# In the last row block, the first branch's sum of each column part is made ahead of the second branch's sum of the part before

## The chip, the cores and the metric

The kernel runs on one core of one Trainium2 chip. The metric is the device time in microseconds (us) of that core. All runs quoted are runs of the same program start to finish. Several runs of a kernel are told as their median, with the lowest and the highest.

A profile gives the span from the first to the last instruction, about 1.3 us shorter than the time. The views print times to 0.01 us. The distances behind PE's last matmul are taken from the ns of the trace and then rounded, so one can be 0.01 off the difference of two printed times. PE is TensorE (matmuls), ACT is ScalarE, DVE is VectorE, SP is the engine that issues most DMA transfers.

## The reference, cut to what matters

Two linear-attention branches, A and B, of the same shape are computed from the same 2048 x 640 input. A gate made from the input mixes them.

```python
x = A_x                                   # (1, 2048, 640) bf16
g = sigmoid((x * gate_w).sum(-1, keepdims=True))
a = branch(x, A_wqkv, A_wo)               # linear attention, then @ wo
b = branch(x, B_wqkv, B_wo)
return g * a + (1 - g) * b
```

By the time the output is made, the kernel has folded everything of a branch but the scaled query features into one 640 x 640 matrix `WP`. A block of 128 output rows is therefore `g * (PQ_A @ WP_A) + (1 - g) * (PQ_B @ WP_B)`, each product a sum of five matmuls over 128 features each. There are 16 row blocks.

## The kernel before

A small list scheduler in Python records every operation with what it reads and writes, and orders each engine's instructions before they are emitted. `final` records one row block. For each column part, PE makes A's sum and ACT scales it by `g` into a buffer `TS`. PE then makes B's sum, and DVE adds `(1 - g)` times it to `TS`. The first fifteen row blocks have one part of 640 columns. The last one has three, of 320, 160 and 160 columns, so that the work behind PE's last matmul is small:

```python
def final(t, parts=((0, D),), put=None):
    last = len(parts) > 1
    ...
    for lo, hi in parts:
        n = 1 if hi - lo <= 512 else 2
        w = (hi - lo) // n
        ts = _Tile(1, ring["ts"])                 # one of three TS slots
        ...                                        # o_ap, t_ap: the output and TS slices
        for x, X in enumerate(XS):                 # branch A, then branch B
            tile = _Tile(n)                        # PSUM bank(s)
            ...
            mms("f%s%d" % (X, t), steps, ...)      # PE: five matmuls per bank
            if x == 0:
                sch.op("ACT", lambda e, ...: e.activation(t_ap(), acc(), ACT.Copy, scale=GA[:, 0, t : t + 1]), ...)
            else:
                sch.op("DVE", lambda e, ...: e.scalar_tensor_tensor(
                    out=o_ap(), in0=acc(), scalar=GA[:, 1, t : t + 1], in1=t_ap(), op0=ALU.mult, op1=ALU.add), ...)
        ...                                        # the output transfer, where one is due

final(t, ((0, 320), (320, 480), (480, D)), {320: 0, D: 320})   # the last row block; two output transfers
```

I call the three parts 0, 1 and 2 and the sums A0, B0, A1 and so on. PE makes them in the order A0 B0 A1 B1 A2 B2.

Of the kernel before, what the change touches and what calls it, by code (L numbers as in the profile page):

```python
# [15 lines left out]
ACT = mybir.ActivationFunctionType  # L16
ALU = mybir.AluOpType
# [7 lines left out]
NC = 5  # L25
# [261 lines left out]
def _act_ns(n, psum=True):  # L287
    return n / 1.2 + (52.0 if psum else 94.0)


def _dve_ns(n, rate=1):
    return n / (0.96 * rate) + 68.0
# [6 lines left out]
def bass_gated_mix__linear_attn_block__linear_attn_block__prompt_kernel(nc, A_x, A_wqkv, A_wo, B_x, B_wqkv, B_wo, gate_w, out):  # L299
# [4 lines left out]
    XS = ("A", "B")  # L304

    with ExitStack() as es:
        E = es.enter_context

        def sb(name, shape, dtype=dt.bfloat16):
            return E(nc.sbuf_tensor(name, shape, dtype))  # L310
# [11 lines left out]
        PQ = {X: FE[:, x, :].rearrange("p (k s) -> p k s", s=S) for x, X in enumerate(XS)}  # L322
        WP = {X: sb("WP" + X, [128, NC, D]) for X in XS}
# [12 lines left out]
        GA = sb("GA", [128, 2, NT], dt.float32)  # L336
# [10 lines left out]
        OL = sb("OL", [128, D])  # L347
        OS = sb("OS", [128, NOS, D])
# [3 lines left out]
        PS = E(nc.psum_tensor("ps", [128, 8, 512], dt.float32))  # L352
# [4 lines left out]
        sch = _Sched()  # L357
# [5 lines left out]
        def dma(eng, name, dst, src, reads=(), writes=(), us=1.0, transpose=False, slow=False):  # L363
            n_sem[0] += 1
            sem = E(nc.semaphore(name="d%d_%s" % (n_sem[0], name)))

            def fn(e):
                if slow:
                    with nc.allow_non_contiguous_dma(reason="few elements"):
                        ins = e.dma_start(dst, src)  # L370
                else:
                    ins = e.dma_start(dst() if callable(dst) else dst, src() if callable(src) else src, transpose=transpose)  # L372
                return ins.then_inc(sem, 16)

            return sch.op(eng, fn, us * 1e3, reads=reads, writes=writes, name=name, sem=sem)

        def mms(name, steps, reads, writes, cols, lat=190.0, par=1, prio=None, after=None):


            def fn(pe):  # L380
                ins = None
                for o, l, r, a, z, tp in steps():
                    ins = pe.matmul(o, l, r, start=a, stop=z, tile_position=tp, skip_group_check=True)  # L383
                return ins

            return sch.op("PE", fn, cols / PE_GHZ / par, reads=reads, writes=writes, name=name, lat=lat, prio=prio, after=after)
# [39 lines left out]
        for t0, t1 in ((2, 4), (4, 8), (8, 12), (12, 16)):  # L426
            dma(
                "SP", "xt%d" % t0, XT[:, :, 128 * t0 : 128 * t1], xin[128 * t0 : 128 * t1, :],
                writes=[("XT", t) for t in range(t0, t1)], us=0.82 * (t1 - t0), transpose=True,
# [3 lines left out]
        for t0, t1 in ((2, 4), (4, 8), (8, 12), (12, 16)):  # L433
            dma(
                "SP", "xn_%d" % t0, XN[:, t0:t1, 0:D], xin[128 * t0 : 128 * t1, :].rearrange("(t p) f -> p t f", p=128),
                writes=[("XN", t) for t in range(t0, t1)], us=0.5 * (t1 - t0),
# [49 lines left out]
        ring = {"ek": _Ring(NEK), "dn": _Ring(2), "rx": _Ring(2), "os": _Ring(NOS), "ts": _Ring(NTS)}  # L486
# [335 lines left out]
        def final(t, parts=((0, D),), put=None):  # L822

            last = len(parts) > 1
            os = None if last else _Tile(1, ring["os"])
            row = out[0, 128 * t : 128 * t + 128, :]
            for lo, hi in parts:
                n = 1 if hi - lo <= 512 else 2
                w = (hi - lo) // n
                ts = _Tile(1, ring["ts"])  # L830

                def o_ap(lo=lo, hi=hi, w=w):
                    v = OL[:, lo:hi] if last else OS[:, os.slot, lo:hi]
                    return v.rearrange("p (h f) -> p h f", f=w)

                def t_ap(ts=ts, hi=hi, lo=lo, w=w):
                    return TS[:, ts.slot, 0 : hi - lo].rearrange("p (h f) -> p h f", f=w)

                okey = ("OL", lo) if last else (os,)
                for x, X in enumerate(XS):  # L840
                    tile = _Tile(n)

                    def steps(X=X, tile=tile, lo=lo, w=w, n=n):
                        return [
                            (PS[:, tile.banks[h], 0:w], PQ[X][:, k, 128 * t : 128 * t + 128],
                             WP[X][:, k, lo + w * h : lo + w * h + w], k == 0, k == NC - 1, None)
                            for k in range(NC) for h in range(n)
                        ]

                    def acc(tile=tile, n=n, w=w):  # L850
                        b0 = tile.banks[0]
                        return PS[:, b0 : b0 + n, 0:w]

                    mms(
                        "f%s%d" % (X, t), steps, [("PQS", X, t)] + [("WP", X, k) for k in range(NC)], [(tile,)], 5 * n * (w + 6),
                    )
                    if x == 0:
                        sch.op(
                            "ACT", lambda e, acc=acc, t_ap=t_ap: e.activation(t_ap(), acc(), ACT.Copy, scale=GA[:, 0, t : t + 1]),  # L859
                            _act_ns(hi - lo), reads=[(tile,), ("GA",)], writes=[(ts,)], name="fa%d" % t,  # L860
                        )
                    else:
                        sch.op(
                            "DVE",
                            lambda e, acc=acc, t_ap=t_ap, o_ap=o_ap: e.scalar_tensor_tensor(  # L865
                                out=o_ap(), in0=acc(), scalar=GA[:, 1, t : t + 1], in1=t_ap(), op0=ALU.mult, op1=ALU.add
                            ),
                            _dve_ns(hi - lo), reads=[(tile,), (ts,), ("GA",)], writes=[okey], name="fb%d" % t,
                        )
                p0 = (put or {}).get(hi, None if last else 0)  # L870
                if p0 is not None:
                    outs.append(dma(
                        "SP", "out%d_%d" % (t, lo), row[:, p0:hi],
                        (lambda p0=p0, hi=hi: OL[:, p0:hi]) if last else (lambda: OS[:, os.slot, :]),
                        reads=[("OL", c) for c, _ in parts if p0 <= c < hi] if last else [(os,)], us=0.4,
                    ))


        kt = {(X, t): _Tile(2) for X in XS for t in (0, 1)}
# [45 lines left out]
        def finals(b):  # L925
            for t in range(4 * b, 4 * b + 4):
                if t < NT - 1:
                    final(t)
                else:
                    final(t, ((0, 320), (320, 480), (480, D)), {320: 0, D: 320})  # L930
# [51 lines left out]
```

## Time and profile before

| | before |
|---|---|
| time, median of 3 runs | 190.69 us (190.65 to 190.99) |
| span of the profiled run | 189.5 us |
| PE busy | 185.9 us (98%) |
| PE's last matmul ends (modelled) | 187.26 us |
| the last DVE operation starts, ends | 187.51, 187.89 us |
| the last transfer, issue to landing | 1.6 us |

Two lines of the page show what bounds the kernel: the busy times with their shares of the span and the numbers of instructions, and the chain that ended last, by engine.

```profile
PE 185.9 (98%) x1289; PEld 124.0 (65%) x1289; DVE 129.8 (68%) x275; ACT 76.5 (40%) x129; POOL 8.2 (4%) x14
...
PE 94%; DMA 3%; SPq 1%; issue 0%; ACT 0%; DVE 0%; DVEq 0%; ACTq 0%
```

PE is the limit, and its share of the chain equals nearly the whole span. The chain in order of time (start, duration, what) shows where it leaves PE:

```profile
3.55 5.46 DMA WK<-in_B_wqkv_dram
...
9.05 177.88 PE ps L383 x1238
186.93 0.02 issue
186.95 0.02 ACTq L276
186.97 0.04 issue
187.01 0.40 ACT TS L859
187.42 0.03 issue
187.44 0.02 DVEq L276
187.47 0.04 issue
187.51 0.38 DVE OL L865
```

The chain is on PE from 9.05 us, when a weight load lands, until 186.93, when A2's sum ends. It then goes to ACT, which scales A2, and from there to the last DVE operation. Between the links stand short pieces called "issue", and the separate wait instructions (ACTq and DVEq, both L276). PE itself goes on to make B2 meanwhile.

The timeline shows that (start, duration, engine and line, operation, and in brackets the idle time before it with its releaser). A matmul group's start plus its duration is its modelled end.

```profile
186.06 0.51 PE L383 MATMUL ps<-WPB,FE 128*128 128x160 bf16 x5
...
186.41 0.51 PE L383 MATMUL ps<-WPA,FE 128*128 128x160 bf16 x5
...
186.75 0.51 PE L383 MATMUL ps<-WPB,FE 128*128 128x160 bf16 x5
...
187.01 0.39 ACT L859 ACTIVATE TS<-ps,GA 128x160 f32<-128x160 f32 x1 [0.36 <-PE ps L383]
187.51 0.38 DVE L865 SCALAR_TENSOR_TENSOR OL<-ps,GA,TS 128x160 bf16<-128x160 f32 x1 [0.37 <-ACT TS L859]
```

The matmuls of B2 are the line at 186.75 and end at 187.26. The last DVE operation has everything from PE by then and starts only at 187.51, because ACT works on A2 from 187.01 to 187.40. I call the distance from the end of PE's last matmul to the start of the last DVE operation the gap. Here it is 187.51 - (186.75 + 0.51) = 0.25 us. The waits of the last stretch (total, times, longest) put the DVE's largest share there to ACT:

```profile
DVE OL L865 <- ACT TS L859: 0.6, 2, 0.4
DVE OL L865 <- PE ps L383: 0.4, 1, 0.4
```

After DVE there is only the transfer. The view of the output buffer of the last block gives the DVE durations (minimum, median, maximum in ns) and the time to landing:

```profile
L865 DVE SCALAR_TENSOR_TENSOR OL<-ps,GA,TS x3: 383/384/552, 186.0 to 187.5; 128x160 bf16<-128x160 f32 x2, 128x320 bf16<-128x320 f32 x1
...
DMA to landing us min/median/max: 1.6/1.6/1.6
```

The record of an SP transfer lasts 0.33 us, while its landing takes 1.6. The Trainium skill ("Perfetto Trace Analysis", Summary: the profiler window per engine type) says that such a record leaves out the actual data movement. This trace agrees. So a microsecond and a half at the end of the span has no busy engine.

### The profile page before, as it was taken

How to read it: one execution, taken by the hardware profiler on the slowest of the kernel's cores; microseconds unless marked ns; L12 is line 12 of the kernel's file. 1: busy time of each engine (PE TensorE's matmuls, PEld its weight loads, DVE VectorE, ACT ScalarE, POOL GpSimd, SP SyncE). 2: the span in 40 equal slices, each digit the busy share in tenths (PEclk: the TensorE clock that was granted, in tenths of full speed). 3: DMA queues.
4: the chain of work that ended last, by engine and by line, in shares of the span. 5: the costliest groups of instructions: out<-in, count | busy, mean ns of one | idle time of the engine just before them, and what ended most of it. 6: DMA issues, size and time to landing. Idle time of an engine off the chain costs nothing.

```text
span 189.5 us, 3208 instructions
## 1 busy us (share of the span) xinstructions
PE 185.9 (98%) x1289; PEld 124.0 (65%) x1289; DVE 129.8 (68%) x275; ACT 76.5 (40%) x129; POOL 8.2 (4%) x14
## 2 busy tenths in 40 slices
PE   7999999999999999999999999999999999999995
PEld 2555555555788888888855666455556677777774
DVE  1398998999600009996179997898999959933324
ACT  2265656565311122103255478565553422332232
POOL 8900000000000000000000000000000000000000
DMA  5999699991011111112143004675000173221212
GB/s 189 298 243 177 211 388 364 337 231 33 0 35 38 35 35 38 35 35 38 35 95 102 5 22 173 166 224 170 0 0 3 44 226 92 86 89 35 73 69 69
DMA packets 31936, 21.49 MB, mean 113 GB/s; under 512 B 16818, under 2 KB 31666, under 8 KB 31922
## 3 DMA queue, kind: packets, MB, share of 16 engines
q1 hardware_dynamic: 31490, 20.80, 39.5%
q10 hardware_dynamic: 432, 0.49, 0.8%
q8 instruction: 10, 0.16, 0.4%
q14 instruction: 4, 0.03, 0.1%
HBM read 12.05 MB, written 5.31 MB: 92 GB/s over the span
## 4 chain that ended last, share of the span: by engine, by line
PE 94%; DMA 3%; SPq 1%; issue 0%; ACT 0%; DVE 0%; DVEq 0%; ACTq 0%
PE ps L383 94%; DMA WK<-in_B_wqkv_dram 3%; SPq L372 1%; ACT TS L859 0%; DVE OL L865 0%; DVEq L276 0%; ACTq L276 0%
## 5 line engine op out<-in xcount | busy, mean ns | idle before, releaser
L383 PE MATMUL ps<-WK,XT 128*128 128x512 bf16 (+2 forms) x250 | 44.0, 337 | 0.5 <-DMA WK<-in_A_wqkv_dram 0.2
L383 PE MATMUL ps<-XN,FE 128*128 128x320 bf16 x320 | 44.3, 300 | 0.0
L383 PEld LDWEIGHTS ps<-XN,FE 128*128 128x128 bf16 x320 | 37.5, 118 | 5.9
L383 PEld LDWEIGHTS ps<-WK,XT 128*128 128x128 bf16 x250 | 24.1, 98 | 20.0 <-DMA WK<-in_A_wqkv_dram 0.5
L743 ACT ACTIVATE EK<-ps 128x512 bf16<-128x512 f32 x40 | 23.9, 597 | 18.5 <-PE ps L383 16.9
L563 ACT ACTIVATE EK<-ps 128x512 bf16<-128x512 f32 (+1 forms) x42 | 21.4, 526 | 16.2 <-PE ps L383 16.2
L752 DVE SCALAR_TENSOR_TENSOR FE<-ps,EK 128x512 bf16<-128x512 f32 x40 | 26.8, 688 | 0.7
L859 ACT ACTIVATE TS<-ps,GA 128x640 f32<-128x640 f32 (+2 forms) x18 | 13.2, 734 | 29.5 <-PE ps L383 29.5
L383 PE MATMUL ps<-WPB,FE 128*128 128x320 bf16 (+1 forms) x165 | 24.7, 295 | 0.0
L383 PE MATMUL ps<-WPA,FE 128*128 128x320 bf16 (+1 forms) x165 | 24.7, 295 | 0.0
L573 DVE SCALAR_TENSOR_TENSOR FE<-ps,EK 128x512 bf16<-128x512 f32 (+1 forms) x42 | 23.9, 596 | 0.5
L865 DVE SCALAR_TENSOR_TENSOR OS<-ps,GA,TS 128x640 bf16<-128x640 f32 x15 | 13.0, 869 | 14.7 <-PE ps L383 14.7
L383 PE MATMUL ps<-XT,WQA 128*128 128x512 bf16 x100 | 22.8, 380 | 0.0
L383 PE MATMUL ps<-XT,WQB 128*128 128x512 bf16 x100 | 22.7, 379 | 0.0
L600 ACT ACTIVATE GS<-ps 128x640 bf16<-128x640 f32 x10 | 7.0, 704 | 37.0 <-PE ps L383 37.0
L383 PEld LDWEIGHTS ps<-WPA,FE 128*128 128x128 bf16 x165 | 15.9, 98 | 6.1
L383 PEld LDWEIGHTS ps<-WPB,FE 128*128 128x128 bf16 x165 | 15.8, 98 | 6.2 <-ACT TS L859 0.4
L383 PEld LDWEIGHTS ps<-XT,WQB 128*128 128x128 bf16 x100 | 11.7, 117 | 9.1
L383 PEld LDWEIGHTS ps<-XT,WQA 128*128 128x128 bf16 x100 | 11.6, 118 | 9.4 <-issue 0.4
L705 DVE SCALAR_TENSOR_TENSOR GP<-XN,GWB 128x640 bf16<-128x640 bf16 x16 | 13.3, 829 | 4.1 <-PE ps L383 3.6
L811 DVE TENSOR_TENSOR FE<-FE,RX 128x1280 bf16<-128x1280 bf16 (+1 forms) x20 | 12.6, 685 | 1.6 <-DMA RX<-factor 1.6
L567 DVE TENSOR_SCALAR EK<-EK 128x512 bf16<-128x512 bf16 (+1 forms) x42 | 11.4, 272 | 3.1
(52 smaller groups left out, 80.3 us busy)
## 6 DMA issues: line engine op xcount, KB each, us to landing
out_dram<-OS SPq DMA_DIRECT2D x15, 160.0 KB, 1.8
XN<-in_A_x_dram SPq DMA_DIRECT2D x3, 640.0 KB, 8.1
factor<-RC SPq DMA_DIRECT2D x4, 256.0 KB, 2.6
RX<-factor SPq DMA_DIRECT2D x4, 256.0 KB, 3.2
WVA<-in_A_wqkv_dram SPq DMA_DIRECT2D x1, 800.0 KB, 10.4
WQA<-in_A_wqkv_dram SPq DMA_DIRECT2D x1, 800.0 KB, 11.9
WVB<-in_B_wqkv_dram SPq DMA_DIRECT2D x1, 800.0 KB, 11.2
WQB<-in_B_wqkv_dram SPq DMA_DIRECT2D x1, 800.0 KB, 12.5
```

The lines of the kernel that those rows point to most:

```text
L372: ins = e.dma_start(dst() if callable(dst) else dst, src() if callable(src) else src, transpose=transpose)
L383: ins = pe.matmul(o, l, r, start=a, stop=z, tile_position=tp, skip_group_check=True)
L563: "ACT", lambda e, ps=ps, ek=ek: e.activation(ek(), ps(), ACT.Exp), _act_ns(n), reads=[(tile,)], writes=[(es,)],
L567: "DVE", lambda e, ek=ek: e.tensor_scalar(ek(), ek(), 1.0, EPS, op0=ALU.min, op1=ALU.add), _dve_ns(n, 4),
L573: return e.scalar_tensor_tensor(out=out, in0=two(ps()), scalar=0.0, in1=two(ek()), op0=ALU.max, op1=ALU.add)
L600: "ACT", lambda e: e.activation(GS[:, k, :].rearrange("p (h f) -> p h f", f=HALF), pair(tile, HALF), ACT.Copy),
L705: lambda e, t=t: e.scalar_tensor_tensor(out=GP[:, :], in0=XN[:, t, 0:D], scalar=1.0, in1=GWB[:, :], op0=ALU.mult, op1=ALU.mult, accum_out= ...
L743: "ACT", lambda e: e.activation(ek(), PS[:, tile.banks[0], :], ACT.Exp), _act_ns(512), reads=[(tile,)],
L752: lambda e: e.scalar_tensor_tensor(out=dst, in0=PS[:, tile.banks[0], :], scalar=0.0, in1=ek(), op0=ALU.max, op1=ALU.add),
L811: return e.tensor_tensor(out=v, in0=v, in1=RX[:, xs.slot, 512 * x + w * j : 512 * x + w * j + w].unsqueeze(1).to_broadcast([128, NC, w]), ...
L859: "ACT", lambda e, acc=acc, t_ap=t_ap: e.activation(t_ap(), acc(), ACT.Copy, scale=GA[:, 0, t : t + 1]),
L865: lambda e, acc=acc, t_ap=t_ap, o_ap=o_ap: e.scalar_tensor_tensor(out=o_ap(), in0=acc(), scalar=GA[:, 1, t : t + 1], in1=t_ap(), op0=ALU.m ...
```

## The change

The intent: make A's sum of the next part before B's sum of this part, so that ACT's scaling of A runs under PE's other work and the last DVE operation waits for PE alone. PE's order becomes A0 A1 B0 A2 B1 B2. The row blocks with one part stay as they were.

```diff
-            for lo, hi in parts:
+            got = {}
+
+            def total(x, lo, hi):
                 ...
-                ts = _Tile(1, ring["ts"])
+                X = XS[x]
+                tile = _Tile(n)
+                ts = got.setdefault(lo, _Tile(1, ring["ts"]))
                 ...
-                for x, X in enumerate(XS):
-                    tile = _Tile(n)
-                    ...
+                mms("f%s%d" % (X, t), steps, ...)
+                if x == 0:
+                    sch.op("ACT", ...)
+                    return
+                sch.op("DVE", ...)
                 ...                                # the output transfer, as before
+            for i, (lo, hi) in enumerate(parts):
+                if i == 0:
+                    total(0, lo, hi)
+                if i + 1 < len(parts):
+                    total(0, *parts[i + 1])
+                total(1, lo, hi)
```

No operation is added or removed. The built programs differ in the order of the last six groups of matmuls on PE, and the operations of ACT, DVE and SP keep their order.

More of the change, by code (lines that the diff above doesn't have):

```diff
@@ L826, in final, with steps, acc, o_ap @@
             row = out[0, 128 * t : 128 * t + 128, :]
-            for lo, hi in parts:
+            got = {}
+            def total(x, lo, hi):
                 n = 1 if hi - lo <= 512 else 2
                 w = (hi - lo) // n
-                ts = _Tile(1, ring["ts"])
-                def o_ap(lo=lo, hi=hi, w=w):
+                X = XS[x]
+                tile = _Tile(n)
+                ts = got.setdefault(lo, _Tile(1, ring["ts"]))
+                def steps():
+                    return [
+                        (PS[:, tile.banks[h], 0:w], PQ[X][:, k, 128 * t : 128 * t + 128],
+                         WP[X][:, k, lo + w * h : lo + w * h + w], k == 0, k == NC - 1, None)
+                        for k in range(NC) for h in range(n)
+                    ]
+                def acc():
+                    return PS[:, tile.banks[0] : tile.banks[0] + n, 0:w]
+                def o_ap():
@@ L833, in o_ap, with t_ap @@
                     v = OL[:, lo:hi] if last else OS[:, os.slot, lo:hi]
                     return v.rearrange("p (h f) -> p h f", f=w)
-                def t_ap(ts=ts, hi=hi, lo=lo, w=w):
+                def t_ap():
                     return TS[:, ts.slot, 0 : hi - lo].rearrange("p (h f) -> p h f", f=w)
-                okey = ("OL", lo) if last else (os,)
-                for x, X in enumerate(XS):
-                    tile = _Tile(n)
-                    def steps(X=X, tile=tile, lo=lo, w=w, n=n):
-                        return [
-                            (PS[:, tile.banks[h], 0:w], PQ[X][:, k, 128 * t : 128 * t + 128],
-                             WP[X][:, k, lo + w * h : lo + w * h + w], k == 0, k == NC - 1, None)
-                            for k in range(NC) for h in range(n)
-                        ]
-                    def acc(tile=tile, n=n, w=w):
-                        b0 = tile.banks[0]
-                        return PS[:, b0 : b0 + n, 0:w]
-                    mms(
-                        "f%s%d" % (X, t), steps, [("PQS", X, t)] + [("WP", X, k) for k in range(NC)], [(tile,)], 5 * n * (w + 6),
-                    )
-                    if x == 0:
-                        sch.op(
-                            "ACT", lambda e, acc=acc, t_ap=t_ap: e.activation(t_ap(), acc(), ACT.Copy, scale=GA[:, 0, t : t + 1]),
-                            _act_ns(hi - lo), reads=[(tile,), ("GA",)], writes=[(ts,)], name="fa%d" % t,
-                        )
-                    else:
-                        sch.op(
-                            "DVE",
-                            lambda e, acc=acc, t_ap=t_ap, o_ap=o_ap: e.scalar_tensor_tensor(
-                                out=o_ap(), in0=acc(), scalar=GA[:, 1, t : t + 1], in1=t_ap(), op0=ALU.mult, op1=ALU.add
-                            ),
-                            _dve_ns(hi - lo), reads=[(tile,), (ts,), ("GA",)], writes=[okey], name="fb%d" % t,
-                        )
@@ new lines, in total @@
+                mms("f%s%d" % (X, t), steps, [("PQS", X, t)] + [("WP", X, k) for k in range(NC)], [(tile,)], 5 * n * (w + 6))
+                if x == 0:
+                    sch.op(
+                        "ACT", lambda e: e.activation(t_ap(), acc(), ACT.Copy, scale=GA[:, 0, t : t + 1]), _act_ns(hi - lo),
+                        reads=[(tile,), ("GA",)], writes=[(ts,)], name="fa%d" % t,
+                    )
+                    return
+                sch.op(
+                    "DVE",
+                    lambda e: e.scalar_tensor_tensor(
+                        out=o_ap(), in0=acc(), scalar=GA[:, 1, t : t + 1], in1=t_ap(), op0=ALU.mult, op1=ALU.add
+                    ),
+                    _dve_ns(hi - lo), reads=[(tile,), (ts,), ("GA",)], writes=[("OL", lo) if last else (os,)], name="fb%d" % t,
+                )
@@ L873, in final @@
                         "SP", "out%d_%d" % (t, lo), row[:, p0:hi],
-                        (lambda p0=p0, hi=hi: OL[:, p0:hi]) if last else (lambda: OS[:, os.slot, :]),
+                        (lambda: OL[:, p0:hi]) if last else (lambda: OS[:, os.slot, :]),
                         reads=[("OL", c) for c, _ in parts if p0 <= c < hi] if last else [(os,)], us=0.4,
                     ))
+            for i, (lo, hi) in enumerate(parts):
[4 more added lines that the diff above has]
+                total(1, lo, hi)
         kt = {(X, t): _Tile(2) for X in XS for t in (0, 1)}
```

## The prediction

> **What bounds the kernel now.** TensorE. The page's busy table gives PE 185.9 of 189.5 us (98%); the list of cores gives a granted clock of 1.000. The chain that ended last is PE for 94%; in order of time, PE runs in it from 9.05 to 186.93 us without a break. A change that leaves the matmuls as they are can gain only what follows PE's last useful one.
>
> **The tail, all that the change touches.** Timeline of the last stretch: the last row block is made in parts of 320, 160 and 160 columns, in the order A0 B0 A1 B1 A2 B2. Five 160-column matmuls take 0.345 us (starts 186.06, 186.41, 186.75). A2's sum ends at 186.92 by the modelled end; ACT scales it from 187.01 to 187.40; B2's sum ends at 187.26; the last DVE operation starts at 187.51, 0.11 after ACT, and takes 0.38. The output transfer lands 1.6 us after its issue (view of the output tile). So 0.25 us pass between PE's end and the last DVE start, and the wait view puts DVE's waits here down to ACT (0.6 us, two waits).
>
> **What the change does.** It adds and removes no instruction. The built order shows PE's tail as A0 A1 B0 A2 B1 B2; ACT, DVE and SP keep their order. PE should still end near 187.26. The PSUM banks and TS slots that the new order takes were last read by row blocks 13 and 14, over a microsecond earlier, so I expect no new wait on PE.
>
> - A2 ends near 186.58 and ACT is done near 187.05, before B2's end: ACT leaves the critical path.
> - The last DVE then waits for PE. Here DVE starts 0.11 to 0.14 us after its matmuls' modelled end (185.88 to 185.99; 184.52 to 184.66): 187.37 to 187.40, which is 0.11 to 0.14 earlier.
> - Against it: B1 and B2 end 0.345 us apart, and a DVE operation on 160 columns takes 0.384. The Trainium skill ("VectorE: DVE Perf Modes", The DRAIN you can't avoid) says that the next operation does not start until the pipe is empty. Strictly taken, B1's starts near 187.04, B2's not before 187.42, and the gain is 0.09. The trace is milder: two 128x512 operations of 0.688 us fill 1.28 us, so their records overlap by 0.09, and 0.29 us suffices for the small ones. The gain is 0.05 to 0.14 us.
> - B0's sum ends near 186.24, its DVE near 186.90; the block's first output is issued near 186.93 instead of 186.57, and the last one near 187.8. SP's issue takes 0.33 us, so they do not collide.
>
> **Predicted time.** 190.69 - 0.11 = 190.58 us, range 190.25 to 190.90, mostly the scatter of runs (190.65 to 190.99 before). Faster by over 2%: 0.005; within 2%: 0.99; slower: 0.005.
>
> **What would show each step.** PE's last sum ends near 187.26 without new idle time; ACT's last operation ends before 187.15; the chain of waits goes from PE to the last DVE operation with no ACT link; the last DVE starts at 187.37 to 187.46; the last transfer still takes 1.6 us.
>
> **What would make it wrong.** PE stalling at B1, whose first matmul now carries a wait on ACT; DVE still busy with B1 when B2 is ready; the two closer output transfers delaying each other; a shift of whole runs by 0.3 us, more than the gain.

## More of the kernel before

An operation that has to wait for two engines gets its waits in the order in which the scheduler expects them to be met:

```python
o.waits = sorted(lean.values(), key=lambda d: d.end)
...
for d in o.waits:
    ... engobj.wait_ge(sems[d.eng], d.count)       # L276
ins = o.fn(engobj)
```

In the built program the first of them sits on the operation itself. The second becomes an instruction of its own (an EventSemaphore) ahead of the operation.

## The result, and the profile after

| | before | after |
|---|---|---|
| time, median of 6 runs | 190.67 us (190.61 to 190.99) | 190.66 us (190.22 to 191.05) |
| span of the profiled run | 189.5 us | 189.7 us |
| PE's last matmul ends | 187.26 us | 187.60 us |
| gap | 0.25 us | 0.11 us |
| last DVE operation ends, after PE's end | 0.63 us | 0.49 us |
| last transfer, issue to landing | 1.6 us | 1.6 us |
| end of the span, after PE's end | 2.28 us | 2.14 us |

The ratio after to before is 0.9997, with a 95% interval of 0.9979 to 1.0014. The interval is about 0.67 us wide, so it can neither show nor exclude a gain of 0.14.

The profiled run of the changed kernel was, as it happens, one of its longest, and its span is 0.2 us longer than the one before. Its chain says why, and says at the same time that the change did what it should:

```profile
3.55 5.80 DMA WK<-in_B_wqkv_dram
...
9.39 177.87 PE ps L383 x1241
187.26 0.03 issue
187.29 0.02 DVEq L276
187.31 0.04 issue
187.36 0.30 DVE OL L862
187.66 0.04 issue
187.70 0.38 DVE OL L862
```

First, PE's unbroken stretch began at 9.39 us instead of 9.05, because a load of weights landed later. That part of the kernel is not touched by the change. From there to the end of the last matmul PE took the same time in both: 187.26 - 9.05 = 178.21 us before, 187.60 - 9.39 = 178.21 us after. Second, there is no ACT in the chain any more. It goes from B1's sum to B1's DVE operation and on to the last one. The timeline:

```profile
186.40 0.51 PE L383 MATMUL ps<-WPA,FE 128*128 128x160 bf16 x5
186.67 1.42 DVE L862 SCALAR_TENSOR_TENSOR OL<-ps,GA,TS 128x320 bf16<-128x320 f32 x3 [0.79 <-PE ps L383]
...
186.74 0.86 PE L383 MATMUL ps<-WPB,FE 128*128 128x160 bf16 x10
187.00 0.39 ACT L856 ACTIVATE TS<-ps,GA 128x160 f32<-128x160 f32 x1 [0.62 <-PE ps L383]
187.25 1.20 SPq L372 DMA_DIRECT2D out_dram<-OL  x2
```

The line at 186.74 holds B1 and B2, ten matmuls that end at 187.60. ACT's last operation ran from 187.00 to 187.40, done 0.20 us before that. The DVE line holds three operations and ends at 188.09, so the last of them, of 0.38, starts at 187.70. The waits of the last stretch confirm it: DVE waits for PE there, and the two waits for ACT are gone.

```profile
DVE OL L862 <- PE ps L383: 0.8, 1, 0.8
```

```profile
L862 DVE SCALAR_TENSOR_TENSOR OL<-ps,GA,TS x3: 384/384/551, 186.7 to 187.7; 128x160 bf16<-128x160 f32 x2, 128x320 bf16<-128x320 f32 x1
...
DMA to landing us min/median/max: 1.6/1.6/1.6
```

The DVE operations and the transfer are as long as before. The tail is 0.14 us shorter, and nothing after PE's end gives it back: the span ends 2.14 us after PE instead of 2.28. The start of the program moved by 0.34 us in the other direction in this pair of profiles.

### The profile page after: what moved, and what is told of

It reads as the page before. It is cut to its first block, busy times and chain, and to the rows that moved or that the text cites. A ratio compares the mean times of both kernels' runs of the same rounds, so it can differ in the third digit from the quotient of the medians.

```text
span 189.7 us, 3209 instructions
## 1 busy us (share of the span) xinstructions
PE 186.3 (98%) x1289; PEld 124.0 (65%) x1289; DVE 130.1 (69%) x275; ACT 76.4 (40%) x129; POOL 8.2 (4%) x14
## 4 chain that ended last, share of the span: by engine, by line
PE 94%; DMA 3%; SPq 1%; DVE 0%; issue 0%; DVEq 0%
PE ps L383 94%; DMA WK<-in_B_wqkv_dram 3%; SPq L372 1%; DVE OL L862 0%; DVEq L276 0%
```

## The experiments

The theory, called ACT in the expectations: the change takes ACT's step off the chain and does nothing else, so it gains what the last DVE operation lost by waiting for ACT, 0.14 us. That is below what the start of the program varies by from run to run. The rivals:

- ORDER: the new order of the sums, or their closer spacing, lets DVE start sooner whatever ACT does.
- DVE: the last DVE operation now waits for DVE itself to be free.
- OUT: putting off the first output transfer gives part of the gain back in the last one.

All experiments change only the last row block. I judge them by the gap and by the end of the last DVE operation, both counted from the end of PE's last matmul in the same profile. That takes the scatter of the start out.

### 1. The old order without the wait for ACT

```diff
+                tr = tp if lo == 480 else ts      # tp: the TS slot of the part before
+                tp = ts
 ...
-    in1=t_ap(), ... reads=[(tile,), (ts,), ("GA",)]
+    in1=r_ap(), ... reads=[(tile,), (tr,), ("GA",)]   # r_ap: the slice of slot tr
```

The last DVE operation adds the TS slot that ACT had filled for part 1. The result is wrong in the last 160 columns of the last block (a relative error of 0.14). ACT's last operation still runs, but nobody waits for it.

> The old order A0 B0 A1 B1 A2 B2, but the last DVE operation adds the slot that ACT filled for the second part, so that it no longer needs ACT's last operation (wrong values in 160 columns, on purpose). Gap = start of the last DVE operation less the modelled end of the last matmul; before 0.25 us, after 0.10. Theory ACT (the change gains by taking ACT's step off the chain, nothing else): gap 0.10. Rival ORDER (two B sums in a row, or their closer spacing, let DVE start sooner, ACT or not): gap stays 0.25.

Measured: PE ends at 187.24, the last DVE operation starts at 187.28, and the gap is 0.04 us. The end of the chain:

```profile
187.25 0.03 issue
187.28 0.38 DVE OL L870
```

With PE's order untouched, taking ACT's link away shortens the gap by more than the change does. ORDER falls: it expected 0.25. But my own number of 0.10 was missed too. In this chain there is no DVEq piece between PE and DVE. DVE had met its wait for part 1's ACT operation earlier, so the last operation needed one wait instead of two. That became the subject of experiments 10 and 12.

### 2 and 3. ACT's last operation done twice, in the old and in the new order

```diff
-    sch.op("ACT", ... ACT.Copy, scale=GA[:, 0, t : t + 1] ...)
+    for _ in range(2 if lo == 480 else 1): sch.op("ACT", ... ACT.Copy, scale=GA[:, 0, t : t + 1] ...)
```

> The old order with ACT's last operation done twice (same values). ACT is on the chain: the gap should grow by one dependent ACT step, 0.39 us and some 0.05 of semaphore, from 0.25 to about 0.70. If ACT was not what the last DVE operation waited for, the gap stays at 0.25 or grows by less than 0.2.

> The new order with ACT's last operation done twice. After, ACT was done 0.21 us before PE's end and 0.31 before the last DVE start. Theory ACT: of the 0.45 us added, 0.2 is hidden in that slack; ACT ends some 0.24 after PE's end, gap about 0.35, against about 0.70 in the old order with the same doubling. Rival DVE (the last DVE operation starts when DVE is free of the one before, whatever ACT does): gap stays 0.10.

Measured: in the old order PE ends at 187.52 and the last DVE operation starts at 188.19, so the gap is 0.67 us. In the new order PE ends at 187.04, DVE starts at 187.37, and the gap is 0.33. The chain in the old order, then in the new:

```profile
187.27 0.40 ACT TS L859
...
187.70 0.40 ACT TS L859
...
188.19 0.38 DVE OL L865
```

```profile
186.45 0.40 ACT TS L856
...
186.88 0.40 ACT TS L856
...
187.37 0.38 DVE OL L862
```

Both runs came out as theory ACT expected, within 0.03 us. The same extra ACT operation costs 0.67 - 0.25 = 0.42 us in the old order and 0.33 - 0.11 = 0.22 us in the new one. The difference, 0.20 us, is what the new order hides: after, ACT was done 0.20 us before PE's end. Rival DVE, which expected 0.10 whatever ACT does, falls in that form: with ACT late enough, the chain goes through ACT again. Whether DVE's spacing still holds the last operation of the changed kernel itself is a question for experiments 5, 6 and 8.

### 4. Only the last A sum moved

```diff
-                if i == 0:
-                    total(0, lo, hi)
-                if i + 1 < len(parts):
-                    total(0, *parts[i + 1])
+                if i < 2:
+                    total(0, lo, hi)
+                if i == 1 and len(parts) > 2:
+                    total(0, *parts[2])
                 total(1, lo, hi)
```

The order is A0 B0 A1 A2 B1 B2. The first output transfer is not put off.

> Order A0 B0 A1 A2 B1 B2: only the last A sum is moved, the first output is not put off. Theory ACT: gap 0.10 as after; first output issued 0.69 us before PE's end as before (after: 0.35). Rival OUT (putting off the first output gives part of the gain back in the last transfer): the last transfer, from issue to the span's end, is shorter here than after by 0.1 us or more; theory ACT: the same within 0.05, 1.6 us to landing.

Measured: PE ends at 186.88, the last DVE operation starts at 186.98, and the gap is 0.11 us, as after the change. The first output was issued at 186.18, 0.70 us before PE's end, against 0.35 after the change (187.25 and 187.60). The last transfer took 1.6 us to its landing in both, and the span ended 2.14 us after PE in both. OUT falls, and moving one sum is all that the gain needs.

### 5 and 6. Two parts of 320 columns, in the old and in the new order

```diff
-final(t, ((0, 320), (320, 480), (480, D)), {320: 0, D: 320})
+final(t, ((0, 320), (320, D)), {320: 0, D: 320})
```

> The last row block in two parts of 320 columns, old order A0 B0 A1 B1. ACT on 320 columns takes 0.53 us and B1's sum 0.68, so ACT should be done before B1 ends: gap 0.11 already in the old order, no ACT link in the chain; the DVE operation takes 0.55 instead of 0.38. If the old order as such costs a wait, the gap is 0.2 or more.

> The same two parts in the new order A0 A1 B0 B1. Theory ACT: nothing to gain, gap 0.11 as in the old order within 0.03 (the two B sums end 0.68 apart, DVE's first operation takes 0.55, so DVE is free). Rival ORDER: gap shorter than in the old order by 0.1 or more.

Measured: in the old order PE ends at 187.51 and DVE starts at 187.62; in the new order 187.63 and 187.74. The gap is 0.11 us in both, and both chains go from PE to DVE without ACT. In the last 320 columns of the old order, ACT started at 186.87 and took 0.53 us, so it was done 0.11 before PE. The new order gains nothing where B's sum is longer than ACT's step. The larger last DVE operation (0.55 us) makes the end 0.66 after PE, slightly worse than before.

### 7 and 8. Parts of 320, 160, 80 and 80 columns, in the old and in the new order

```diff
-final(t, ((0, 320), (320, 480), (480, D)), {320: 0, D: 320})
+final(t, ((0, 320), (320, 480), (480, 560), (560, D)), {320: 0, D: 320})
```

> Parts of 320, 160, 80, 80, old order. An 80-column sum should take about 0.18 us (0.345 for 160, scaled with 6 columns of overhead), ACT on 80 columns about 0.32 and DVE 0.30 (from 0.39 and 0.53; 0.38 and 0.55, extrapolated). Theory ACT: ACT starts 0.09 after A3's end, so the gap is 0.09 + 0.32 - 0.18 + 0.11 = 0.34; larger if ACT is still busy with A2. Then the last DVE operation ends about 0.64 after PE, no better than before (0.63).

> The same four parts, new order A0 A1 B0 A2 B1 A3 B2 B3. ACT has one 0.18 us sum less to hide in. Theory ACT with the DVE overlap of the trace (0.04 to 0.09 us): B1's DVE operation starts 0.10 after its sum, at 0.44 before PE's end, B2's at PE's end at the earliest about -0.08, B3's about 0.2 after that: gap 0.10 to 0.20, DVE limits, not ACT; the last DVE operation ends 0.40 to 0.50 after PE (after: 0.48). If ACT still limits, the gap is 0.25 or more.

Measured: in the old order PE ends at 186.81 and the last DVE operation starts at 187.16, a gap of 0.35 us, end 0.65 after PE. In the new order PE ends at 187.60 and DVE starts at 187.75, a gap of 0.15, end 0.44 after PE. The smaller B's sum is against ACT's step, the more the new order is worth: 0 for 320 columns, 0.14 for 160, 0.20 for 80. In the new order with 80 columns DVE begins to limit. The end of its chain goes from one DVE operation to the next:

```profile
187.53 0.14 DVE OL L862
187.67 0.08 issue
187.75 0.29 DVE OL L862
```

An operation of 0.30 us began at 187.53 (the chain counts it only up to 187.67), and the next one began 0.22 us later. ACT had been done 0.08 us before that next one began. My prediction feared this effect for the change itself. Here it shows with the last two sums 0.18 us apart; with 0.345 it did not.

### 9. The changed kernel once more, in five rounds

> The changed kernel once more, timed in five rounds. The theory (a gain of 0.15 us in the tail, which the scatter of the start covers) expects a ratio of 0.9985 to 1.0005 with an interval that likely still holds 1; the gap from PE's end to the last DVE start 0.10 again, whatever the span. If the gain is given back somewhere that every run shares, the gap or the last transfer is longer than 0.10 and 1.6 us.

Measured: 190.67 us median (190.38 to 191.06, 6 runs) against 190.80 us (190.33 to 191.04, 11 runs) before, ratio 1.0000 with an interval of 0.9987 to 1.0014. In the profile PE ends at 187.24, the last DVE operation starts at 187.35, the gap is 0.11 us, and the landing takes 1.6. The tail repeats, and the time again tells nothing at this size.

### 10. The changed kernel with the two waits exchanged

```diff
-            o.waits = sorted(lean.values(), key=lambda d: d.end)
+            o.waits = sorted(lean.values(), key=lambda d: d.end, reverse=o.name in ("fa15", "fb15"))
```

Both waits are still made, and the built program has the same order of operations. In the last row block the wait that comes last now sits on the operation, and the one that has long been met sits in the separate instruction.

> The changed kernel, where the last row block's ACT and DVE operations carry their two waits the other way round: in the built program the wait for PE now sits on the operation itself and the wait for the other engine in the separate wait instruction ahead of it. In the run without the ACT wait the gap was 0.04 and not 0.10, and its chain has no separate wait instruction between PE and DVE. If that instruction is what costs 0.06, the gap is 0.04 to 0.06 here; if having two waits at all costs it, 0.10. No time difference that the rounds can tell from the changed kernel: 0.9980 to 1.0005 of before.

Measured: PE ends at 187.15, the last DVE operation starts at 187.19, and the gap is 0.04 us. The end of the chain has no DVEq piece:

```profile
187.17 0.03 issue
187.19 0.38 DVE OL L862
```

The last DVE operation ends 0.42 us after PE, against 0.49 for the changed kernel. Time: 190.54 us median (190.25 to 190.96), ratio to before 0.9993, interval 0.9979 to 1.0007. Having two waits costs nothing; having the late one in the separate instruction costs 0.07 us.

### 11. Four parts with the waits exchanged

The edits of experiments 8 and 10 together.

> Candidate for the shortest tail: four parts (320, 160, 80, 80) in the new order, with the waits the other way round in the last row block. Four parts alone had the last DVE operation end 0.44 after PE (after: 0.48). With 0.05 less per DVE operation: gap 0.09 to 0.12, end 0.38 to 0.42 after PE. In time against before: 0.25 less expected in the mean, ratio 0.9975 to 1.0000.

Measured: PE ends at 188.22, DVE starts at 188.33, the gap is 0.11 us and the end is 0.41 us after PE, against 0.42 with three parts. Time: 190.56 us median (190.25 to 191.58), ratio 0.9993, interval 0.9979 to 1.0007. The profiled run was the one of 191.58 us, with PE waiting for the load until 9.99 us. The end of its chain goes from one DVE operation, at 188.08, to the next, at 188.33. But the timeline shows that ACT was late again:

```profile
187.90 0.33 ACT L856 ACTIVATE TS<-ps,GA 128x80 f32<-128x80 f32 x1 [0.20 <-PE ps L383]
...
188.33 0.30 DVE OL L862
```

ACT's last operation ended at 188.23, after PE's end, and the DVE operation began 0.10 us after it, the same distance as in the kernel before. DVE's own spacing does not explain the start: 0.25 us lie between the two starts, and in experiment 8 0.22 were enough. So in this last part the exchange put the late wait, the one for ACT, into the separate instruction. As tried, four parts gain 0.01 us in the tail over three, in one profile of each; four parts with each late wait on its operation were not tried.

### 12. The old order with the waits exchanged

The edit of experiment 10 on the kernel before.

> The kernel before (old order A0 B0 A1 B1 A2 B2), with the waits of the last row block's ACT and DVE operations the other way round, as in the run on the changed kernel, where the gap fell from 0.10 to 0.03. In the chain before, the last ACT operation came 0.08 after PE and the last DVE operation 0.10 after ACT, each through a separate wait instruction. If each such instruction costs 0.06 to 0.07 where it stands between two links, the gap falls from 0.25 to 0.11 to 0.13, and still goes through ACT. If the last-coming wait's place matters for PE's semaphore alone, only the ACT link shortens: 0.18 to 0.19.

Measured: PE ends at 187.00, the last DVE operation starts at 187.12, and the gap is 0.12 us, still through ACT:

```profile
8.79 177.87 PE ps L383 x1241
186.67 0.02 issue
186.69 0.40 ACT TS L859
187.09 0.02 issue
187.12 0.38 DVE OL L865
```

Both links lost their separate wait instruction. Of the 0.25 us before, 0.13 were two such instructions standing between links. This one-line edit gains nearly as much in the tail as the change does, with no reordering at all.

### All profiles together

| profile | PE's end | gap | last DVE end after PE | load of B's weights, median us to landing | span |
|---|---|---|---|---|---|
| before | 187.26 | 0.25 | 0.63 | 5.2 | 189.5 |
| after | 187.60 | 0.11 | 0.49 | 5.6 | 189.7 |
| 9, after again | 187.24 | 0.11 | 0.49 | 5.2 | 189.4 |
| 4, last A sum only | 186.88 | 0.11 | 0.49 | 4.8 | 189.0 |
| 10, waits exchanged | 187.15 | 0.04 | 0.42 | 5.1 | 189.2 |
| 11, four parts, waits exchanged | 188.22 | 0.11 | 0.41 | 6.1 | 190.3 |
| 12, old order, waits exchanged | 187.00 | 0.12 | 0.50 | 4.8 | 189.1 |

The gap repeats to 0.01 us between profiles of one order and one way of waiting, while PE's end varies by 1.3 us in this table. In nine profiles (before, after, 3, 5, 6, 9, 10, 11 and 12) the chain starts with the load of B's key weights, and PE's stretch from there to its last matmul takes 178.18 to 178.23 us. In 3, 9, 10 and 11 the chain cuts this stretch by nine pieces of "issue", nearly all of 0.05 or 0.06 us; nine matmul records are missing from each of these traces. So in those nine profiles the scatter of PE's end comes from the time before PE's stretch, which starts at 8.79 to 9.99 us. In the other five the chain starts differently, with the first input rows (1 and 2) or with PE's first operations (4, 7 and 8), and I did not take the scatter apart further. Why the same load lands after 4.7 us in one run and 6.1 in another stays open.

## Why the prediction was right

- **What bounds the kernel.** Right. PE's work is unchanged by the change, 178.21 us from the start of PE's stretch, when the load has landed, to the last matmul in both profiles.
- **No new wait on PE.** Right. PE showed no idle time among the reordered sums, although B1's first matmul carries a wait for an older ACT operation.
- **ACT leaves the chain.** Right, and shown: ACT is done 0.20 us before PE's end (expected: 187.05 against 187.26, or 0.21), and the chain after has no ACT link. It passes through B1's DVE operation, which I had not written. The record of that operation runs on past the start of the last one, so the view finds no idle time on DVE to put down to PE; the next point shows that it is PE that the last operation waits for. Experiments 1 and 5 show that the old order as such costs nothing when ACT is not late. Experiments 2 and 3 show that the new order hides 0.20 us of ACT's work and no more.
- **The size.** I gave 0.05 to 0.14 us with 0.11 in the middle, and the gap fell by 0.14 us in both profiles of the changed kernel, the upper end. The term that was mis-sized is DVE's spacing between B1 and B2. The strict reading allowed only 0.09 of gain, and I went to the middle between the readings. With sums 0.345 us apart, the last operation of the changed kernel starts 0.11 after PE's end. That is the same as in experiments 5 and 6, where DVE was certainly free, so DVE does not hold it back. Its record begins 0.04 us before that of B1's operation ends, while operations that ran back to back in the kernel before overlap by about 0.08. So the strict reading was wrong, and the milder one from the trace fits, though no run here has two operations of 0.38 us at its 0.29 us from start to start. Experiment 8 showed DVE limiting at closer sums, 0.22 us for an operation of 0.30, which is an overlap of 0.08.
- **The outputs.** Right. The first output was issued 0.35 us before PE's end (expected 0.33), the landing of the last stayed at 1.6 us, and experiment 4 found no cost in putting the first one off.
- **The time.** 190.66 us lies in the range. But the kernel before, at 190.67, lies in that range too, so the hit says more about scatter than about the change. The measured difference of the medians is 0.01 us, not 0.11, and the rounds' interval holds both. I named a shift of whole runs by 0.3 us as what would hide the gain. The two profiles showed just that: PE began its stretch 0.34 us later.
- **What I did not see.** I read the 0.11 us from PE's end to DVE's start as a fixed latency. It is 0.04 us plus 0.07 for the wait instruction between them, which can be moved out of the way.

A version that beats both kernels in the tail is number 10: 0.42 us from PE's end to DVE's end, against 0.63 and 0.49. In time it is not shown to be faster than either; its interval of 0.9979 to 1.0007 holds 1.

## What to carry to other kernels

Once one engine is busy for 98% of the span, reordering other engines' work can win only in the short stretches where it does not run, here the one behind its last instruction. Bound the gain there from the timeline before writing the change, and judge it by distances inside the profile, counted from that engine's end, when it is smaller than the scatter of whole runs. Moving a producer's step one sum earlier pays only as far as it outlasts the sum that it hides under: nothing at 320 columns, 0.14 us at 160, 0.20 at 80. And where an operation waits for two engines, look at which wait stands in the separate instruction, and put the one that is met early there. Which one that is can change with the size of the parts, as experiment 11 shows.

## What the Trainium skill lacked or had wrong

- "Perfetto Trace Analysis", Identifying Dependency Chains, says that an instruction waiting on several engines may have EventSemaphore instructions inserted before it. The built programs and the chains here agree. It doesn't say what that costs, nor that it matters which wait is put there: 0.07 us for one link (gap 0.11 with the late wait in the separate instruction, 0.04 with the early one there), and 0.13 us for two links in the old order (0.25 and 0.12).
- "VectorE: DVE Perf Modes", The DRAIN you can't avoid, says that the next operation does not start until the pipe is empty. The same paragraph adds that one that is not held starts earlier, which my prediction left out, so the page is not wrong here. That section gives no figure for how much the records of a profile then overlap: an operation with a record of 0.30 us was followed by the next one 0.22 us after its start (experiment 8), and two 128x512 operations of 0.688 us filled 1.28 us in the kernel before. No run here tells what the pipe itself does in between.
- I know of no page that says how much the landing of one and the same load varies from run to run. In these runs, B's key weights landed after 4.7 to 6.1 us (median of its issues, by profile), and the start of PE's unbroken stretch moved with it, from 8.79 to 9.99 us in the nine profiles where it could be read.
